# Window attention issued in the written order on four engines, as a pipeline of query steps

## Chip, cores and metric

The kernel runs on one core of one Trainium2 chip. The time is that of one execution on the device, in microseconds (us). The kernel before was run three times: 968.87, 969.32 and 969.57 us, median 969.32.

## What is computed

Causal attention over a window of 128 positions, with a linear bias per head, on 4 batches of 8 heads, 576 positions and head size 64. Then two feed-forward networks (FFNs) on the 2304 tokens, 512 to 2048 to 512, the first with a sigmoid gate and the second with a clipped square. The weights come as 64-bit floats.

```python
scores = q @ k.T / 8 - slope[h] * |i - j|      # only 0 <= i - j < 128, else -1e9
attn = exp(scores - max);  attn = attn / (sum(attn) + 1e-9)
x = (attn @ v) as (2304, 512)
h = x @ w1_in;  x = (h / (1 + exp(-1.702 h))) @ w1_out
h = x @ w2_in;  out = where(h >= 1, h, where(h <= -1, 0, (h + 1)**2 / 4)) @ w2_out
```

## The kernel before

Attention goes by **units**: one batch and two heads, 16 units. A unit has 9 groups of 64 queries, taken two at a time in five **steps** (m = 0 to 4; the last has one group), so there are 80 steps in all. A group's queries of both heads fill the 128 rows, and its keys are a strip of up to 192 columns (64 and 128 in a unit's first two groups).

Per unit, `trans_qk` (three chunks c) transposes q and k on TensorE and copies them out of PSUM: k on VectorE (DVE, line 206), q on ScalarE (ACT) or DVE (line 209). Per step, `scores` runs the score matmuls (line 220), then on DVE one operation that adds the bias, scales and takes the row's extreme (line 228), and on ACT the exp with its row sum (line 231). `norm` inverts the row sums on DVE (an add and a reciprocal, lines 238 and 239) and multiplies the probabilities on GpSimd (POOL, line 242). `trans_p` transposes the probabilities on TensorE and copies them out on ACT (lines 257 to 267). Per unit, `pv_unit` multiplies with v on TensorE (lines 281 to 287) and copies the result on ACT (line 288) and DVE (line 289) into `xt`, the activations that the FFN reads. The probabilities rotate through five buffers `pbuf`.

Beside attention, the first nine of 16 weight slices of the first FFN are loaded (`load_w1`, two halves each, 18 halves). A half is a DMA, five DVE operations that turn 64-bit floats into 32-bit ones (lines 65 to 73), a cast on ACT (line 75) and a subtraction on GpSimd (line 77) that leaves the rest, so that a value is kept as two parts.

The order of the work comes from keys. `at(key, fn, ...)` collects events, and they are traced in the order of their keys, counted in steps. What is traced is then put into each engine's queue by the planner of the language, which has a cost model and may put a later instruction that it holds ready ahead of an earlier one that waits. DMAs are issued by SyncE (SP), in a queue of their own. After the events, `split_block` cuts the first 462 tokens of `xt` into two parts for the FFN (ACT line 106, DVE line 107). In the FFN, every product of two such values is three matmuls (high by high, and twice high by low): `stage_h` (line 337) fills `ph`, ACT and DVE make `gs` (lines 343 to 351), and `stage_o` (lines 389 and 391) runs two stages behind. The other seven slices, and those of the second FFN, are loaded within the FFNs.

Of the kernel before, what the change touches and what calls it, by code (L numbers as in the profile page):

```python
# [25 lines left out]
def tile_window_attention_two_ffn(ctx: ExitStack, tc: tile.TileContext, q, k, v, w1_in, w1_out, w2_in, w2_out, out):  # L26
# [30 lines left out]
    def load_half(src, w, i, in_ffn=False):  # L57
        raw = stage.tile([P, 512, 2], I32, tag="raw", name="raw")
        if i == 0:
            nc.sync.dma_start(out=raw.rearrange("p (c f) t -> p c (f t)", c=KC), in_=src)  # L60
        else:
            nc.sync.dma_start(out=raw.rearrange("p f t -> p (f t)"), in_=src)
        lo, hi = raw[:, :, 0], raw[:, :, 1]
        x = stage.tile([P, 512], I32, tag="x", name="x", bufs=2)
        nc.vector.tensor_scalar(out=x, in0=hi, scalar1=0x7FFFFFFF, scalar2=None, op0=ALU.bitwise_and)
        nc.vector.tensor_scalar(
            out=f32(x), in0=f32(x), scalar1=HI_MIN, scalar2=HI_MAX, op0=ALU.max, op1=ALU.min)
        finish_late()
        nc.vector.tensor_scalar(
            out=x, in0=x, scalar1=3, scalar2=0x3FFFFFF8, op0=ALU.logical_shift_left, op1=ALU.bitwise_and)  # L70
        nc.vector.scalar_tensor_tensor(  # L71
            out=x, in0=lo, scalar=29, in1=x, op0=ALU.logical_shift_right, op1=ALU.bitwise_or)
        nc.vector.scalar_tensor_tensor(  # L73
            out=x, in0=hi, scalar=SIGN_TOP, in1=x, op0=ALU.bitwise_and, op1=ALU.bitwise_or)
        nc.scalar.copy(w[:, 0, i, :], f32(x))  # L75
# [18 lines left out]
    def load_w1(f, i):  # L94
        if i == 0:
            w1[f] = new_slice(w_a)
        load_weights(w1_in, w1_out, f, w1[f], (i,))
# [14 lines left out]
    with ExitStack() as actx:  # L112
# [80 lines left out]
        def trans_qk(u, c):  # L193
# [4 lines left out]
            ps = ps_a.tile([P, 2, 256], F32, tag="a", name="ps_qk")  # L198
            n = 256 if c < 2 else 64
            for i in range(2):  # L200
                for t in range(0, n, P):
# [3 lines left out]
                        ident[0:r, 0:r])  # L205
            nc.vector.tensor_copy(d["k"][:, 256 * c:256 * c + n], ps[:, 1, 0:n])
# [8 lines left out]
        def scores(u, m):  # L215
            b, hp = units[u]
            d = st[u]
            ps = ps_s.tile([P, 2, 256], F32, tag="s", name="ps_s")
            for e, i, lo in groups(m):
                nc.tensor.matmul(  # L220
                    ps[:, e, lo:192], d["q"][:, i, :], d["k"][:, 64 * i - 128 + lo:64 * i + 64], start=True, stop=True)
            n = NM * u + m
            assert n < len(pbuf) or n - len(pbuf) in done
            pt = d["p", m] = pbuf[n % len(pbuf)]
            sm = d["sm", m] = st_p.tile([P, 3, 2], F32, tag="sm", name="sm")
            for e, i, lo in groups(m):
# [3 lines left out]
                    scale=-0.125, scalar=3.0e38, accum_out=sm[:, 0, e:e + 1])  # L230
                nc.scalar.activation(  # L231
                    x, x, AF.Exp, bias=sm[:, 0, e:e + 1], scale=-1.0, accum_out=sm[:, 1, e:e + 1])

        def norm(u, m):
            d = st[u]
            sm, pt = d["sm", m], d["p", m]
            nn = len(groups(m))
            nc.vector.tensor_scalar_add(sm[:, 2, 0:nn], sm[:, 1, 0:nn], 1e-9)
            nc.vector.reciprocal(sm[:, 2, 0:nn], sm[:, 2, 0:nn])  # L239
            for e, i, lo in groups(m):  # L240
                x = pt[:, e, 64 * e + lo:64 * e + 192]
                nc.gpsimd.tensor_scalar(  # L242
                    out=x, in0=x, scalar1=sm[:, 2, e:e + 1], scalar2=1.0, op0=ALU.mult, op1=ALU.mult)

        def trans_p(u, m):
# [3 lines left out]
            if m == 0:  # L249
                d["pt"] = pt_p.tile([P, 4 * NM, P], F32, tag="pt", name="pt")  # L250
            pt = d["pt"]
            ps = ps_t.tile([P, 4, P], F32, tag="t", name="ps_t")
            n = 4 * m
            if m < NM - 1:
# [4 lines left out]
                if m > 0:  # L259
                    nc.scalar.copy(pt[:, n - 2:n + 2, :], ps)  # L260
                else:
                    nc.scalar.copy(pt[:, n:n + 2, :], ps[:, 2:4, :])  # L262
            else:
                nc.tensor.transpose(ps[:, 0, :], p[:, 0, 0:128], ident)  # L264
                nc.tensor.transpose(ps[0:64, 1, :], p[:, 0, 128:192], ident)
                nc.scalar.copy(pt[:, n - 2, :], ps[:, 0, :])
                nc.scalar.copy(pt[0:64, n - 1, :], ps[0:64, 1, :])

        def pv_unit(u):
            b, hp = units[u]  # L270
            d = st[u]
            pt, vr = d["pt"], d["v"]
            t0 = b * S
            heads = [slice(64 * j, 64 * j + 64) for j in range(2)]
            x = ps_x.tile([P, 512], F32, tag="x", name="ps_x")
            x1 = ps_a.tile([P, 2, 256], F32, tag="a", name="ps_x1")
# [11 lines left out]
            nc.scalar.copy(xt[hp][:, t0:t0 + 512], x)  # L288
            nc.vector.tensor_copy(xt[hp][:, t0 + 512:t0 + S], x1[:, 0, 0:64])
# [181 lines left out]
```

## Time and profile before

| | |
|---|---|
| median of 3 runs | 969.32 us |
| profiled execution | 969.63 us, span 967.8 us |
| busy: TensorE, weight loads | 954.2 us (99%), 841.2 us (87%) |
| busy: DVE, ACT, POOL | 564.9 us (58%), 383.5 us (40%), 99.2 us (10%) |
| first FFN matmul | 155.34 us from the span's start |

The profile is of one execution. Times in it count from the span's start. "Busy" is the time in which an engine had an instruction in work; instructions overlap at their ends, so the sum of durations is over the busy time, and a stretch that is shown as busy need not be dense. "Idle before" is the time in which the engine had nothing in work ahead of an instruction, with the releaser that ended it. PEld is TensorE's loading of weights (the stationary operand), PE its matmuls.

### The profile page before, as it was taken

To read this page: it belongs to the slowest core of one execution; us is meant where nothing else is said; L and a number is where in the kernel's file an instruction comes from. 1 tells how busy PE (TensorE), PEld (TensorE's weight loads), DVE (VectorE), ACT (ScalarE), POOL (GpSimd) and SP (SyncE) were. 2 spreads that over 40 slices of the span, in tenths; PEclk is the share of its full clock that TensorE was granted. 3 is DMA by queue.
4 is the path that set the end of the run, shared out by engine and by line. 5 is a ranking of instruction groups with operands and counts; after the bars stand their busy time and mean duration, and the time that the engine had idled before them with its cause. 6 is when DMAs were issued, how large, how long until landed. Compare 5 with 4: busy or idle time off the path is not lost.

```text
span 967.8 us, 13767 instructions
## 1 busy us (share of the span) xinstructions
PE 954.2 (99%) x5024; PEld 841.2 (87%) x5024; DVE 564.9 (58%) x1449; ACT 383.5 (40%) x928; POOL 99.2 (10%) x186
## 2 busy tenths in 40 slices
PE   7999999999999999999999999999999999999998
PEld 5878876888998989999888898899999999999997
DVE  5799999997323322422489999943443434444443
ACT  5999996333223222322333433332322422323322
POOL 4566664000000000000000000000000000000000
PEclk9999999999999999999999999999999999999999
DMA  5666644443000000000024333100000000000000
GB/s 135 156 156 163 154 124 121 131 131 109 1 1 1 1 1 1 1 0 1 1 80 133 118 105 113 63 33 1 17 16 1 33 1 1 33 1 1 33 1 33
DMA packets 81971, 53.32 MB, mean 55 GB/s; under 512 B 58992, under 2 KB 75632, under 8 KB 81904
## 3 DMA queue, kind: packets, MB, share of 16 engines
q1 hardware_dynamic: 81760, 52.31, 18.9%
q8 instruction: 40, 0.66, 0.3%
q14 instruction: 27, 0.22, 0.1%
q10 hardware_dynamic: 144, 0.13, 0.0%
HBM read 47.71 MB, written 4.72 MB: 54 GB/s over the span
## 4 chain that ended last, share of the span: by engine, by line
PE 93%; DVE 3%; SPq 1%; ACT 1%; DMA 1%; issue 0%; POOL 0%; POOLq 0%; ACTq 0%; DVEq 0%
PE ph L337 39%; PE o L389 21%; PE o L391 19%; PE ps_s L220 5%; PE ps_x L281 3%; PE ps_qk L203 2%; PE ps_t L257 1%; PE ps_t L258 1%; DVE x L73 1%; DVE x L71 1%; DMA raw<-in_moe_w_out_dram 0%; PE ps_x L287 0%; PE ps_t L264 0%; DVE w L79 0%; DVE ph L347 0%
## 5 line engine op out<-in xcount | busy, mean ns | idle before, releaser
L337 PE MATMUL ph<-xs,w 128*128 128x384 f32 (+2 forms) x2112 | 431.2, 353 | 0.0
L337 PEld LDWEIGHTS ph<-xs,w 128*128 128x128 f32 x2112 | 385.2, 188 | 28.7
L391 PE MATMUL o<-w,gs 128*128 128x512 f32 x864 | 216.5, 395 | 1.1 <-ACT gs L350 1.1
L389 PE MATMUL o<-gs,w 128*128 128x460 f32 (+1 forms) x960 | 213.8, 371 | 1.1 <-ACT gs L350 1.1
L389 PEld LDWEIGHTS o<-gs,w 128*128 128x128 f32 x960 | 180.5, 188 | 21.8 <-ACT gs L350 1.5
L391 PEld LDWEIGHTS o<-w,gs 128*128 128x128 f32 x864 | 161.0, 188 | 32.2 <-ACT gs L350 2.0
L350 ACT CAST gs<-ph 128x384 fp32r<-128x384 f32 (+2 forms) x176 | 89.7, 510 | 169.3 <-DVE ph L348 110.5
L351 DVE TENSOR_TENSOR gs<-ph,gs 128x384 fp32r<-128x384 f32 (+2 forms) x176 | 104.3, 593 | 73.4 <-ACT gs L350 73.1
L347 DVE TENSOR_TENSOR ph<-ph,ga 128x384 f32<-128x384 f32 x96 | 54.3, 565 | 143.4 <-ACT ga L346 143.4
L344 DVE TENSOR_TENSOR ph<-ph,ga 128x460 f32<-128x460 f32 (+1 forms) x80 | 51.4, 643 | 140.0 <-ACT ga L343 140.0
L346 ACT ACTIVATE ga<-ph,half 128x384 f32<-128x384 f32 x96 | 55.8, 582 | 155.2 <-PE ph L337 149.1
L343 ACT ACTIVATE ga<-ph 128x460 f32<-128x460 f32 (+1 forms) x80 | 44.4, 555 | 173.2 <-PE ph L337 173.1
L242 POOL TENSOR_SCALAR p<-p,sm 128x192 f32<-128x192 f32 (+1 forms) x144 | 70.0, 497 | 59.6 <-DVE sm L239 17.8
L231 ACT ACTIVATE p<-p,sm 128x192 f32<-128x192 f32 (+1 forms) x144 | 62.0, 433 | 8.9 <-DVE sm L228 8.5
L220 PE MATMUL ps_s<-kt,q 128*128 128x192 f32 (+2 forms) x288 | 60.4, 333 | 0.0
L75 ACT CAST w<-x 128x512 fp32r<-128x512 f32 x64 | 39.5, 620 | 44.8 <-DVE x L73 43.5
L348 DVE SCALAR_TENSOR_TENSOR ph<-ga,ph 128x384 f32<-128x384 f32 x96 | 53.8, 561 | 2.7
L228 DVE CUSTOM_DVE_ANT_0 p<-ps_s,bias 128x192 f32<-128x192 f32 (+1 forms) x144 | 44.9, 329 | 13.2 <-PE ps_s L220 8.9
L220 PEld LDWEIGHTS ps_s<-kt,q 128*128 128x128 f32 x288 | 45.3, 199 | 5.7 <-ACT pt L262 2.7
L71 DVE SCALAR_TENSOR_TENSOR x<-raw,x 128x512 int32<-128x512 int32 x64 | 45.1, 708 | 0.5
L73 DVE SCALAR_TENSOR_TENSOR x<-raw,x 128x512 int32<-128x512 int32 x64 | 44.7, 702 | 0.4
L281 PE MATMUL ps_x<-pt,vraw 128*64 128x256 f32 (+1 forms) x256 | 39.1, 366 | 0.3 <-ACT xt L288 0.3
(58 smaller groups left out, 589.0 us busy)
## 6 DMA issues: line engine op xcount, KB each, us to landing
raw<-in_moe_w_in_dram SPq DMA_DIRECT2D x32, 512.0 KB, 3.7
raw<-in_moe_w_out_dram SPq DMA_DIRECT2D x32, 512.0 KB, 3.5
out_dram<-ob SPq DMA_DIRECT2D x17, 256.0 KB, 2.0
vraw<-in_v_dram SPq DMA_DIRECT2D x32, 128.0 KB, 2.5
qkraw<-in_q_dram SPq DMA_DIRECT2D x30, 128.0 KB, 2.7
qkraw<-in_k_dram SPq DMA_DIRECT2D x30, 128.0 KB, 2.6
qkraw<-in_q_dram SPq DMA_DIRECT2D x16, 32.0 KB, 2.4
qkraw<-in_k_dram SPq DMA_DIRECT2D x16, 32.0 KB, 2.5
```

What stands on the lines that cost most here:

```text
L71: nc.vector.scalar_tensor_tensor(out=x, in0=lo, scalar=29, in1=x, op0=ALU.logical_shift_right, op1=ALU.bitwise_or)
L73: nc.vector.scalar_tensor_tensor(out=x, in0=hi, scalar=SIGN_TOP, in1=x, op0=ALU.bitwise_and, op1=ALU.bitwise_or)
L220: nc.tensor.matmul(ps[:, e, lo:192], d["q"][:, i, :], d["k"][:, 64 * i - 128 + lo:64 * i + 64], start=True, stop=True)
L231: nc.scalar.activation(x, x, AF.Exp, bias=sm[:, 0, e:e + 1], scale=-1.0, accum_out=sm[:, 1, e:e + 1])
L242: nc.gpsimd.tensor_scalar(out=x, in0=x, scalar1=sm[:, 2, e:e + 1], scalar2=1.0, op0=ALU.mult, op1=ALU.mult)
L281: nc.tensor.matmul(x[r, 128 * kb:128 * kb + 64 * n].rearrange("p (a b) -> p a b", b=64), vr[:, kb, r], pt[:, 4 * kb:4 * kb + n, r], start= ...
L337: nc.tensor.matmul(ph, w[f][:, a, 0, c * P:(c + 1) * P], xs[j][c][:, b, :], start=(c == 0 and i == 0), stop=(c == KC - 1 and i == 2))
L346: nc.scalar.activation(a, ph, AF.Relu, scale=0.5, bias=half)
L350: nc.scalar.copy(gs[:, 0, :], ph)
L351: act_last[0] = nc.vector.tensor_tensor(out=gs[:, 1, :], in0=ph, in1=f32(gs[:, 0, :]), op=ALU.subtract)
L389: nc.tensor.matmul(o[j][m][:, 0:n], w[f][:, a, 1, sl], gs[:, b, :], start=first, stop=last)
L391: nc.tensor.matmul(o[j][m], gs[:, b, sl], w[f][:, a, 1, :], start=first, stop=last)
```

## The change

Only the attention part is touched. All instructions of the events on TensorE, ACT, DVE and GpSimd are issued in the order in which they are traced, so the keys are now the order of these four queues. SyncE stays with the planner, and `setup` before the events and `split_block` behind them are outside.

The functions are cut so that each event has, by and large, the work of one engine at one point: `trans_qk` and `move_qk`, `scores` and `softmax`, `trans_p` and `move_p`, `pv_unit` and `move_x`. The keys move: scores one step ahead of their softmax, q/k transposes from 5u-1.58 to 5u-2.6, `trans_p` from s+3.5 to s+4.2, `pv_unit` from 5u+12.05 to 5u+13.2, loads of q/k from 5u-2.87 to 5u-4.6, loads of v from 5u-13.98 to 5u+3.5. The row sums of two steps share one small tile and are inverted together (`invert`), after which both steps are normalised; a unit's fifth step is inverted alone. A weight half becomes a generator in six pieces that are 0.55 step apart, and halves follow each other every 3.95 steps in place of 4.725.

```diff
-    def load_half(src, w, i, in_ffn=False):
+    def half_pieces(src, w, i, in_ffn=False):
...
         nc.vector.tensor_scalar(out=x, in0=hi, scalar1=0x7FFFFFFF, scalar2=None, op0=ALU.bitwise_and)
+        yield
...
+    def load_half(*args):
+        for _ in half_pieces(*args):
+            pass
...
+        def softmax(u, m):
...
+            if m % 2 == 0:
+                d["sm"] = st_p.tile([P, 3, 2, 2], F32, tag="sm", name="sm")
+            sm = d["sm", m] = d["sm"]
...
+        def invert(u, m):
+            d = st[u]
+            sm = d["sm", m].rearrange("p a b c -> p a (b c)")
+            nn = 4 if m < NM - 1 else 1
             nc.vector.tensor_scalar_add(sm[:, 2, 0:nn], sm[:, 1, 0:nn], 1e-9)
             nc.vector.reciprocal(sm[:, 2, 0:nn], sm[:, 2, 0:nn])
...
-                at(5 * u - 2.87, load_qk, u)
-                at(5 * u - 13.98, load_v, u)
+                at(5 * u - 4.6, load_qk, u)
+                at(5 * u + 3.5, load_v, u)
             for c in range(3):
-                at(5 * u - 1.58 + c * 1.49 if u > 0 else -99 + c, trans_qk, u, c)
+                key = 5 * u - 2.6 + c * 1.49 if u > 0 else -99 + c
+                at(key, trans_qk, u, c)
+                at(key + 0.45, move_qk, u, c)
             for m in range(NM):
                 s = 5 * u + m
-                at(s, scores, u, m)
-                at(s + 0.74, norm, u, m)
-                at(s + 3.5, trans_p, u, m)
-            at(5 * u + 4 + 8.05, pv_unit, u)
+                at(s - 1.0, scores, u, m)
+                at(s, softmax, u, m)
+                if m % 2 or m == NM - 1:
+                    at(s + 1.3, invert, u, m)
+                    at(s + 1.35, norm, u, m)
+                    if m % 2:
+                        at(s + 1.34, norm, u, m - 1)
+                at(s + 4.2, trans_p, u, m)
+                at(s + 4.7, move_p, u, m)
+            at(5 * u + 13.2, pv_unit, u)
+            at(5 * u + 14.1, move_x, u)
         for f in range(SPLIT):
             for i in range(2):
-                at(19.59 + 9.45 * (f + 0.5 * i), load_w1, f, i)
-        for key, _, fn, args in sorted(ev, key=lambda e: e[:2]):
-            fn(*args)
+                g = load_w1(f, i)
+                for n in range(6):
+                    at(19.59 + 3.95 * (2 * f + i) + 0.55 * n, next, g, None)
+        with tc.manual_schedule(engines={mybir.EngineType.PE, mybir.EngineType.Activation, mybir.EngineType.DVE,
+                                         mybir.EngineType.Pool}):
+            for key, _, fn, args in sorted(ev, key=lambda e: e[:2]):
+                fn(*args)
```

## Rows read from the trace of the kernel before

**Rows 1.** The page, busy time of each engine, its share, and instructions.

```profile
PE 954.2 (99%) x5024; PEld 841.2 (87%) x5024; DVE 564.9 (58%) x1449; ACT 383.5 (40%) x928; POOL 99.2 (10%) x186
```

**Rows 2.** Windows: stretch, length, busy PE, PEld, DVE, ACT, POOL (instructions), clock, DMA, GB/s.

```profile
18.70:26.60 7.90, 7.90 (x56) 6.03 (x55) 5.45 (x35) 7.76 (x29) 3.92 (x10) 1.00 0.73 158
43.60:132.50 88.90, 88.90 (x688) 70.75 (x687) 81.99 (x402) 83.37 (x293) 57.87 (x101) 1.00 0.63 157
...
200.00:240.00 40.00, 40.00 (x192) 35.89 (x191) 35.55 (x69) 15.10 (x27) 0.00 (x0) 1.00 0.38 120
240.00:968.00 728.00, 722.70 (x3542) 650.80 (x3540) 355.56 (x653) 216.98 (x404) 0.00 (x0) 1.00 0.08 27
```

**Rows 3.** Timeline at the FFN's start: start, duration, engine, line, count, idle before.

```profile
155.34 7.83 PE L337 MATMUL ph<-xs,w 128*128 128x462 f32 x36
...
164.28 2.80 PE L389 MATMUL o<-gs,w 128*128 128x462 f32 x12 [1.10 <-ACT gs L350]
```

**Rows 4.** Timeline of ACT within one unit, 90 to 98 us.

```profile
90.56 0.57 ACT L260 COPY pt<-ps_t 128x512 f32<-128x512 f32 x1
...
91.02 0.46 ACT L231 ACTIVATE p<-p,sm 128x192 f32<-128x192 f32 x1
...
91.47 0.45 ACT L231 ACTIVATE p<-p,sm 128x192 f32<-128x192 f32 x1
...
91.91 0.58 ACT L288 COPY xt<-ps_x 128x512 f32<-128x512 f32 x1
...
92.38 0.28 ACT L266 COPY pt<-ps_t 128x128 f32<-128x128 f32 x1
...
92.69 0.63 ACT L75 CAST w<-x 128x512 fp32r<-128x512 f32 x1
...
94.10 0.75 ACT L209 COPY q<-ps_qk 64x256 f32<-64x256 f32 x2
...
97.23 0.35 ACT L231 ACTIVATE p<-p,sm 128x64 f32<-128x64 f32 x1 [0.67 <-DVE sm L228]
```

**Rows 5.** Groups of DVE by line and shape, 43.6 to 132.5 us; last row 180 to 240.

```profile
L238 DVE TENSOR_SCALAR sm<-sm 128x2 f32<-128x2 f32 x40 | 7.7, 193 | 0.5 <-ACT p L231 0.5
L65 DVE TENSOR_SCALAR x<-raw 128x512 int32<-128x512 int32 x10 | 7.4, 743 | 0.0
L71 DVE SCALAR_TENSOR_TENSOR x<-raw,x 128x512 int32<-128x512 int32 x10 | 7.2, 722 | 0.0
L239 DVE RECIPROCAL sm<-sm 128x2 f32<-128x2 f32 x40 | 6.2, 155 | 0.1
L228 DVE CUSTOM_DVE_ANT_0 p<-ps_s,bias 128x64 f32<-128x64 f32 x11 | 2.4, 219 | 2.8 <-PE ps_s L220 1.7 <-POOL p L242 1.0
...
L65 DVE TENSOR_SCALAR x<-raw 128x512 int32<-128x512 int32 x13 | 5.5, 423 | 0.7 <-DMA raw<-in_moe_w_in_dram 0.6
```

**Rows 6.** The same view of ACT, 43.6 to 132.5 us: the exps.

```profile
L231 ACT ACTIVATE p<-p,sm 128x192 f32<-128x192 f32 x70 | 31.4, 452 | 1.3 <-DVE sm L228 1.3
...
L231 ACT ACTIVATE p<-p,sm 128x64 f32<-128x64 f32 x10 | 3.5, 348 | 2.1 <-DVE sm L228 2.0
```

**Rows 7.** Line 77 on GpSimd: ns min/median/max, first and last start in us.

```profile
L77 POOL TENSOR_TENSOR w<-x,w x18: 1262/1279/1716, 44.8 to 169.8; 128x512 fp32r<-128x512 f32 x18
```

**Rows 8.** Timeline of DVE at the start.

```profile
8.92 2.92 DVE L152 SCALAR_TENSOR_TENSOR bias<-rel,mask 64x192 bf16<-64x192 f32 x8
...
12.48 0.22 DVE L228 CUSTOM_DVE_ANT_0 p<-ps_s,bias 128x64 f32<-128x64 f32 x1
```

**Rows 9.** Timeline of DVE at the end of attention.

```profile
147.01 0.35 DVE L228 CUSTOM_DVE_ANT_0 p<-ps_s,bias 128x192 f32<-128x192 f32 x1
...
153.15 3.90 DVE L107 TENSOR_TENSOR xs<-xt,xs 128x462 fp32r<-128x462 f32 x3
```

**Rows 10.** Timeline of GpSimd and DVE at one weight half, 95 to 97 us.

```profile
95.05 1.72 POOL L77 TENSOR_TENSOR w<-x,w 128x512 fp32r<-128x512 f32 x1
...
95.67 1.38 DVE L69 TENSOR_SCALAR x<-x 128x512 int32<-128x512 int32 x1
```

More of the change, by code (lines that the diff above doesn't have):

```diff
@@ L96, in load_w1 @@
             w1[f] = new_slice(w_a)
-        load_weights(w1_in, w1_out, f, w1[f], (i,))
+        src = w1_out[f * P:(f + 1) * P, :]
+        if i == 0:
+            src = w1_in.rearrange("(c p) f -> p c f", p=P)[:, :, 2 * f * P:2 * (f + 1) * P]
+        yield from half_pieces(src, w1[f], i)
     NX = max(B1 + B2)
@@ L205, in trans_qk, with move_qk @@
                         ident[0:r, 0:r])
+        def move_qk(u, c):
+            d = st[u]
+            ps, n = d["ps", c], 256 if c < 2 else 64
             nc.vector.tensor_copy(d["k"][:, 256 * c:256 * c + n], ps[:, 1, 0:n])
@@ L215, in scores @@
         def scores(u, m):
-            b, hp = units[u]
             d = st[u]
-            ps = ps_s.tile([P, 2, 256], F32, tag="s", name="ps_s")
+            ps = d["s", m] = ps_s.tile([P, 2, 256], F32, tag="s", name="ps_s")
             for e, i, lo in groups(m):
@@ L221, in scores @@
                     ps[:, e, lo:192], d["q"][:, i, :], d["k"][:, 64 * i - 128 + lo:64 * i + 64], start=True, stop=True)
+        def softmax(u, m):
+            b, hp = units[u]
+            d = st[u]
+            ps = d["s", m]
             n = NM * u + m
@@ L229, in scores @@
                     out=x, in0=ps[:, e, lo:192], in1=bias[:, hp, lo:192], op0=ALU.add, op1=ALU.min,
-                    scale=-0.125, scalar=3.0e38, accum_out=sm[:, 0, e:e + 1])
+                    scale=-0.125, scalar=3.0e38, accum_out=sm[:, 0, m % 2, e:e + 1])
                 nc.scalar.activation(
-                    x, x, AF.Exp, bias=sm[:, 0, e:e + 1], scale=-1.0, accum_out=sm[:, 1, e:e + 1])
+                    x, x, AF.Exp, bias=sm[:, 0, m % 2, e:e + 1], scale=-1.0, accum_out=sm[:, 1, m % 2, e:e + 1])
+        def invert(u, m):
+            d = st[u]
+            sm = d["sm", m].rearrange("p a b c -> p a (b c)")
+            nn = 4 if m < NM - 1 else 1
+            nc.vector.tensor_scalar_add(sm[:, 2, 0:nn], sm[:, 1, 0:nn], 1e-9)
+            nc.vector.reciprocal(sm[:, 2, 0:nn], sm[:, 2, 0:nn])
         def norm(u, m):
@@ L258, in trans_p @@
                     nc.tensor.transpose(ps[:, 2 + e, :], p[:, e, 128:256], ident)
[L259 to L262, printed above, removed]
             else:
@@ L265, in trans_p, with move_p @@
                 nc.tensor.transpose(ps[0:64, 1, :], p[:, 0, 128:192], ident)
+        def move_p(u, m):
+            d = st[u]
+            if m == 0:
+                d["pt"] = pt_p.tile([P, 4 * NM, P], F32, tag="pt", name="pt")
+            pt, ps, n = d["pt"], d["t", m], 4 * m
+            if m == 0:
+                nc.scalar.copy(pt[:, n:n + 2, :], ps[:, 2:4, :])
+            elif m < NM - 1:
+                nc.scalar.copy(pt[:, n - 2:n + 2, :], ps)
+            else:
                 nc.scalar.copy(pt[:, n - 2, :], ps[:, 0, :])
@@ L269, in pv_unit @@
         def pv_unit(u):
-            b, hp = units[u]
             d = st[u]
             pt, vr = d["pt"], d["v"]
-            t0 = b * S
             heads = [slice(64 * j, 64 * j + 64) for j in range(2)]
-            x = ps_x.tile([P, 512], F32, tag="x", name="ps_x")
-            x1 = ps_a.tile([P, 2, 256], F32, tag="a", name="ps_x1")
+            x = d["x"] = ps_x.tile([P, 512], F32, tag="x", name="ps_x")
+            x1 = d["x1"] = ps_a.tile([P, 2, 256], F32, tag="a", name="ps_x1")
             last = NM - 1
@@ L287, in pv_unit, with move_x @@
                 nc.tensor.matmul(x1[r, 0, 0:64], vr[0:64, last, r], pt[0:64, 4 * last - 1, r], start=False, stop=True)
-            nc.scalar.copy(xt[hp][:, t0:t0 + 512], x)
-            nc.vector.tensor_copy(xt[hp][:, t0 + 512:t0 + S], x1[:, 0, 0:64])
+        def move_x(u):
+            b, hp = units[u]
+            d = st[u]
+            t0 = b * S
+            nc.scalar.copy(xt[hp][:, t0:t0 + 512], d["x"])
+            nc.vector.tensor_copy(xt[hp][:, t0 + 512:t0 + S], d["x1"][:, 0, 0:64])
         ev = []
```

18 lines of the change are left out of this document (7 added, 11 removed).

## Prediction

> **What bounds the kernel now.** I read the page first: TensorE shows 99% of the span busy [rows 1], which alone says nothing, since it is drawn busy in attention and in the FFNs alike. So I read the windows next [rows 2]. In the FFN stretches weight loads (PEld) fill 35.89 of 40 us and the matmul count is steady (192 in 40 us; 3542 in 728 us, 4.87 per us). That is TensorE at its own pace, nothing in the diff touches it, and it begins at 155.34 us [rows 3]. In the ten attention units from 43.60 to 132.50 the same column is only 70.75 of 88.90, while ACT is busy 83.37 and DVE 81.99 [rows 2]. So the span is 155.3 us of attention in front of an 812 us FFN stretch, and only the first part, with its seam to the second, can move.
>
> A rule of the Trainium skill bears on that column. It (Perfetto Trace Analysis, section "Identifying the Most-Contended Engine") says that matmul busy share is a bad measure of how near TensorE is to its limit, and that busy weight loads tell more. The two rows above agree, 80% against 90%. By the matmul column alone nothing could be gained in attention, which is rival 1.
>
> Next I read the timeline of ACT in one unit, to get what an instruction costs there from its start to the start of the next [rows 4]. A 192-wide exp with its sum read takes 0.45 us (91.02 to 91.47), a 512-wide copy 0.46 (90.56 to 91.02), the output copy 0.47 (91.91 to 92.38), the two last small copies 0.31 together (92.38 to 92.69), two q copies 0.75. One unit is 7 wide exps 3.15, the 64-wide 0.35, the 128-wide about 0.40, three wide copies 1.38, the 256-wide copy about 0.27 (between the small and the wide ones), the two small 0.31, three q copies 1.12, the output copy 0.47: together 7.45 us. A weight half adds one cast, 0.63 less the 0.10 by which such copies overlap the next, 0.52. The stretch ran one half per unit (10 in 88.9 us [rows 5]), so ACT needed 7.97 of the 8.89 us that a unit took. **ACT is the nearest bound, and 0.92 us per unit are lost to waits.** Of these the profile shows 3.4 us in ten units as idle time before exps, nearly all for DVE, and 2.1 of it in front of the first, 64-wide exp of a unit [rows 6]. DVE itself sat idle 2.8 us before that same first step, 1.7 of it for the score matmuls [rows 5]: a unit's first scores come just in time, after transposes and copies of q and k.
>
> **The change, part by part.**
>
> *Lead.* Scores are issued one step before their softmax, q/k transposes about one step earlier (key 5u-2.6 for 5u-1.58), and their copies become events of their own. This takes away the wait at a unit's start. In the other places DVE still feeds ACT, but the order now lets DVE be about a step ahead. I take the 0.34 us of shown waits as gone, and 0.1 of the hidden rest: 0.92 becomes about 0.47. Bounds: 0.1 (all hidden) and over 0.92 (rival 2). What then is late next is DVE itself.
>
> *Row sums for two steps.* Per unit five adds and five reciprocals become three of each. They last 0.193 and 0.155 us [rows 5], so four fewer save DVE at most 0.70 us of busy time; much of such a duration overlaps the next, so I take 0.4, lower end 0.28. The inversion now stands behind both exps of the pair, so the even step is normalised about 1.6 steps later (key 2.34 for 0.74). GpSimd waits, the transposes of that step behind it are moved from 3.5 to 4.2, and after the later normalisation 1.9 steps (3 us) remain for some 1.7 us of GpSimd work. I cost that wait at nothing; if its cover goes, TensorE's transposes, the copies and the probability buffer five steps on stall by the excess, up to one weight subtraction (1.28 us at the median [rows 7]).
>
> *Weights.* Halves come every 3.95 steps instead of 4.725, cut into six pieces. From step 20 to 80 that is 15.2 halves in 12 units, 1.27 a unit instead of 1. ACT: +0.27 x 0.52 = 0.14. GpSimd: +0.27 x 1.28 = 0.35, against 57.87 busy of 88.90. DVE: a half is three single-input operations and two two-input ones; undisturbed, as later in the FFN, the first kind takes 0.42 and the second about 0.7, 2.7 us in all, and here up to 0.74 and 0.72, 3.7 us [rows 5]. I take 3.2, so +0.86 us per unit (0.7 to 1.0). DVE goes from 8.20 busy to 8.20 - 0.4 + 0.86 = 8.66, though that column counts stalls and overlaps. The five DVE pieces are spread 0.55 step apart, so a step waits behind one or two pieces, not five. What is gained is at the far end: in before the subtractions of these halves run until 169.8 us [rows 7], far into the FFN.
>
> *Unit time.* ACT 7.45 + 1.27 x 0.52 = 8.11, plus waits 0.47, is 8.58; I take **8.6 us**, which also sits at the DVE figure. Units 0 to 3 carry no weights: ACT 7.45, and the window of unit 1, also without, took 7.90 [rows 2]. I take 7.75 (7.6 to 7.9) for each of units 1 to 3.
>
> *Start.* The first step's DVE operation is at 12.48, behind 2.92 us of bias set-up that began at 8.92 [rows 8]. Whether the set-up now precedes the first copies, the trace can't tell; 10.5 to 12.5, I take 11.8. The first unit has no copies of probabilities to do: 5.8 us (it took 6.2).
>
> *Loads.* SyncE is not in the list of ordered engines, so its queue stays with the planner. Loads of q and k keep three buffers, and those of v still wait for the product two units back, which is 1.15 steps later in the order now (13.2 for 12.05) with its own use later by as much; in the first units q and k go ahead of v, which favours the start. I cost it at nothing; if v were late TensorE would wait at the product, and everything behind it with it.
>
> *Tail.* In before the last step's DVE operation starts at 147.01 and the first FFN matmul at 155.34, 8.3 us later. Now behind the last step stand five copies, the output of unit 14 and the product of unit 15, about 7.2 us through ACT and the single output bank; and on DVE 13 weight pieces, about 8 us, with the split of the first token block last in the written order. In before the planner drew its DVE part forward, three subtractions of 1.3 us each from 153.15 [rows 9]; if it may not do so past the ordered region, the FFN is held up to 10 us after the last step. I take 8.4.
>
> *FFN seam.* TensorE waited 1.10 us for gs at 164.28 [rows 3], while weight halves left from attention occupied DVE. These are gone: -1.1, and -0.4 for a slightly slower pace until 240 us (192 in 40 us against 4.87 per us is under 3 matmuls). Together 1.5 us.
>
> **Sum.** 11.8 + 5.8 + 3 x 7.75 + 11.8 units x 8.6 (steps 20 to 79) = 142.3 us for the last step; + 8.4 = 150.7 for the FFN, against 155.3: 4.6 us. With the seam 6.1 us. The profiled run took 969.63 with a span of 967.8, and the median of the three runs is 969.32; 969.4 - 6.1 = **963.3 us**.
>
> **Rivals.**
>
> 1. *TensorE, or ACT and DVE together, already bound a unit at 8.9 to 9.1 us.* For: the full matmul column, and ACT and DVE both over 92% busy [rows 2]. Against: the PEld share. With 9.0 a unit the last step is 4.7 us later: 968.0, no difference.
>
> 2. *Strict order on DVE makes it the bound (slower).* In before a blocked weight operation is followed by whatever is ready. Now a softmax step queued behind a piece waits for it, and behind a pair's inversion DVE waits for ACT's second exp. A 512-wide DVE operation took 1.38 us instead of 0.42 while GpSimd ran its 1.72 us subtraction [rows 10], and the first exp of a unit, next in line behind it, found ACT idle for 0.67 us [rows 4]. With 1.27 such blocks of 0.95 us per unit unhidden, over the 8.3 to 8.4 us of the rest, a unit takes about 9.6 us: 963.3 + 11.8 x 1.0 = 975.1. It is slower than before from a unit of 9.1 us on, and measurably from 9.3. The Trainium skill (SBUF — State Buffer, section "Who interferes with whom") has the rule for it: the port pair that VectorE and GpSimd share is an exclusive lock, and the loser blocks for the whole instruction. The 1.38 us row agrees with it. Against the rival: six short pieces instead of a run of five, and a step of lead.
>
> 3. *The pipeline runs at ACT's pace.* 8.2 a unit, start at 10.5, first unit 5.5, then 7.6 each, tail 7.2: 135.6 + 7.2 = 142.8, 12.5 us earlier, with the seam 14: 955.4.
>
> **How the numbers follow.** Forecast (959 to 967) 0.55; rival 3 0.12; rival 1 0.15; rival 2 0.18. Under 0.2%, 1.9 us, a measurement of this kernel can't be told from no change: faster 0.67, same 0.15, slower 0.18. The range reaches from most of the way to rival 3 up to the mild half of rival 2: 957 to 972, which leaves about 0.07 below and 0.13 above.
>
> **What would show it.** Right: the first FFN matmul near 151 us; units from the fourth on spaced 8.6 us; idle time before the 64-wide exp near zero; no weight subtraction on GpSimd after the FFN's first microseconds; no wait for gs near the FFN's start. Wrong: units over 9 us with exps waiting for DVE behind weight pieces (rival 2); GpSimd's normalisation as what transposes wait for (pair inversion); a gap between the last product and the first FFN matmul (tail); or a first FFN matmul that moves while the end doesn't.

## Result and profile after

The changed kernel is slower: 979.08 us at the median of three runs (978.85, 979.08, 981.16), against 969.32 us; the ratio is 1.0108 [1.0085, 1.0131]. The profiled run took 978.85 us with a span of 977.1. The forecast was 963.3 us, so it missed by 15.8 us and on the other side of no change; its range ended at 972.

The page of the kernel after, the line that answers to [rows 1]:

```profile
PE 948.7 (97%) x5024; PEld 839.4 (86%) x5024; DVE 561.6 (57%) x1385; ACT 384.3 (39%) x928; POOL 103.7 (11%) x186
```

64 DVE instructions are gone with the inversions, and every other count is the same. As before, this line can't say where the time went. The time stamps of a unit's first step and of the FFN's first matmul can. The table lays both profiles side by side (us from the span's start):

| | before | after | after less before |
|---|---|---|---|
| first step of unit 4 | 43.6 | 42.2 | -1.4 |
| first step of unit 15 (11 units later) | 141.5 | 147.3 | +5.8 |
| last step | 147.01 | 153.16 | +6.15 |
| first FFN matmul | 155.34 | 166.04 | +10.70 |
| end of the span | 967.8 | 977.1 | +9.3 |

So units 0 to 3 gained 1.4 us, the 11 units with weights lost 7.2 (9.55 us each for 8.90), the last unit 0.3, the **tail** (last step to FFN) 4.6 (12.9 for 8.3), and the FFN gained 1.4 (811.1 for 812.5). The windows show the two parts that lost, with the columns of [rows 2]. First the kernel before, over the same 11 units and the tail:

```profile
43.60:141.50 97.90, 97.90 (x756) 77.74 (x755) 89.61 (x442) 91.62 (x322) 64.28 (x112) 1.00 0.62 156
147.00:155.30 8.30, 7.34 (x62) 4.15 (x60) 8.16 (x23) 6.60 (x19) 6.35 (x7) 1.00 0.42 113
```

Then the kernel after: the 11 units, the longest of them, and the tail:

```profile
42.20:147.30 105.10, 94.96 (x752) 77.02 (x750) 95.97 (x416) 94.49 (x326) 72.58 (x113) 0.98 0.59 149
70.20:83.00 12.80, 11.03 (x75) 9.07 (x74) 9.60 (x40) 10.02 (x33) 8.33 (x14) 0.87 0.59 157
153.20:166.00 12.80, 8.82 (x64) 5.28 (x64) 8.82 (x20) 6.13 (x19) 7.85 (x10) 0.87 0.39 110
```

Per unit, DVE is busy 95.97 / 11 = 8.72 us and ACT 94.49 / 11 = 8.59, in a unit of 9.55. On average both have over 0.8 us of idle time in a unit, and neither is more than 92% busy. The loss is uneven. Unit 7, the window from 70.2 us, took 12.7 us for 8.7 before, so that 4.0 of the 7.2 us lie in it; the other ten units took 9.23 us in the mean, for 8.91, and in these DVE is idle for 0.59 us and ACT for 0.78. What sets unit 7 apart stands in the last section. What each waited for stands in the groups (line, operation, shape, count, busy us, mean ns, idle before and what ended it). DVE and ACT of the kernel after, 42.2 to 147.3 us, to set beside [rows 5] and [rows 6]:

```profile
L250 DVE CUSTOM_DVE_ANT_0 p<-ps_s,bias 128x192 f32<-128x192 f32 x77 | 24.5, 351 | 3.7 <-PE ps_t L283 2.5 <-POOL p L268 0.4 <-PE ps_t L280 0.3
L74 DVE SCALAR_TENSOR_TENSOR x<-raw,x 128x512 int32<-128x512 int32 x14 | 10.0, 717 | 0.2
L65 DVE TENSOR_SCALAR x<-raw 128x512 int32<-128x512 int32 x15 | 9.7, 645 | 0.0
L260 DVE TENSOR_SCALAR sm<-sm 128x4 f32<-128x4 f32 x22 | 5.6, 252 | 2.8 <-ACT p L253 2.8
...
L253 ACT ACTIVATE p<-p,sm 128x192 f32<-128x192 f32 x77 | 34.5, 450 | 5.7 <-DVE sm L250 5.3
L225 ACT COPY q<-ps_qk 64x256 f32<-64x256 f32 x34 | 12.5, 367 | 3.0 <-DVE q L225 1.1 <-DVE kt L222 1.0 <-PE ps_qk L215 0.5
L253 ACT ACTIVATE p<-p,sm 128x64 f32<-128x64 f32 x11 | 3.8, 350 | 0.6 <-DVE sm L250 0.6
```

The wait that the change was to remove, before a unit's 64-wide exp, is gone (0.6 us, where [rows 6] have 2.1). It came back in front of the wide exps (5.7 for 1.3), and DVE now waits for ACT at the inversion of a pair (2.8). The two engines wait for each other in turn. One such turn, in unit 8, timeline of DVE in the kernel after:

```profile
83.32 0.14 DVE L260 TENSOR_SCALAR sm<-sm 128x1 f32<-128x1 f32 x1
83.49 0.16 DVE L261 RECIPROCAL sm<-sm 128x1 f32<-128x1 f32 x1
83.57 0.44 DVE L71 TENSOR_SCALAR x<-x 128x512 int32<-128x512 int32 x1
83.93 0.20 DVE L222 COPY kt<-ps_qk 128x64 f32<-128x64 f32 x1
84.06 0.45 DVE L225 COPY q<-ps_qk 64x64 f32<-64x64 f32 x2
84.54 0.69 DVE L74 SCALAR_TENSOR_TENSOR x<-raw,x 128x512 int32<-128x512 int32 x1
85.26 0.36 DVE L250 CUSTOM_DVE_ANT_0 p<-ps_s,bias 128x192 f32<-128x192 f32 x1
...
90.69 0.17 DVE L260 TENSOR_SCALAR sm<-sm 128x4 f32<-128x4 f32 x1 [1.07 <-ACT p L253]
```

and of TensorE and ACT in the same stretch:

```profile
80.66 0.82 PE L235 MATMUL ps_s<-kt,q 128*128 128x192 f32 x4
...
85.66 0.46 ACT L253 ACTIVATE p<-p,sm 128x192 f32<-128x192 f32 x1 [1.15 <-DVE sm L250]
...
87.91 0.60 ACT L80 CAST w<-x 128x512 fp32r<-128x512 f32 x1
88.42 0.58 ACT L293 COPY pt<-ps_t 128x512 f32<-128x512 f32 x1
88.90 0.74 ACT L225 COPY q<-ps_qk 64x256 f32<-64x256 f32 x2
89.67 0.46 ACT L253 ACTIVATE p<-p,sm 128x192 f32<-128x192 f32 x1
```

The scores of the step at 85.26 were done at 81.5. From 83.32 on DVE does, in the written order, an inversion, a weight piece, copies of k and q and another weight piece, 1.94 us in which ACT runs dry for 1.15 us. Five microseconds later it is DVE that stands at the pair's inversion for 1.07 us, since ACT still had a cast and copies to do ahead of the exp at 89.67. The pieces that could have filled this wait are queued behind it.

### The profile page after: what moved, and what is told of

Its sections match the earlier page's. It is cut to its first block, busy times and chain, and to the rows that moved or that the text cites. A ratio compares the mean times of both kernels' runs of the same rounds, so it can differ in the third digit from the quotient of the medians.

```text
span 977.1 us, 13644 instructions
## 1 busy us (share of the span) xinstructions
PE 948.7 (97%) x5024; PEld 839.4 (86%) x5024; DVE 561.6 (57%) x1385; ACT 384.3 (39%) x928; POOL 103.7 (11%) x186
## 4 chain that ended last, share of the span: by engine, by line
PE 79%; DVE 10%; ACT 6%; DMA 2%; issue 2%; SPq 0%; POOL 0%; DVEq 0%; POOLq 0%; ACTq 0%
PE ph L382 37%; PE o L436 20%; PE o L434 17%; ACT p L253 3%; DMA raw<-in_moe_w_in_dram 2%; DVE x L74 1%; PE ps_x L308 1%; PE ps_s L235 1%; DVE x L77 1%; DVE p L250 1%; ACT q L225 1%; ACT pt L293 1%; DVE x L65 1%; DVE w L84 1%; DVE x L71 1%
## 5 line engine op out<-in xcount | busy, mean ns | idle before, releaser
L392 DVE TENSOR_TENSOR ph<-ph,ga 128x384 f32<-128x384 f32 x96 | 54.2, 565 | 142.9 <-ACT ga L391 142.9
L268 POOL TENSOR_SCALAR p<-p,sm 128x192 f32<-128x192 f32 (+1 forms) x144 | 74.5, 534 | 39.7 <-ACT p L253 12.9
L253 ACT ACTIVATE p<-p,sm 128x192 f32<-128x192 f32 (+1 forms) x144 | 61.9, 432 | 10.4 <-DVE sm L250 9.9
L250 DVE CUSTOM_DVE_ANT_0 p<-ps_s,bias 128x192 f32<-128x192 f32 (+1 forms) x144 | 42.1, 327 | 7.9 <-PE ps_t L283 6.2
L215 PE MATMUL ps_qk<-ident,qkraw 128*128 128x128 f32 (+1 forms) x160 | 27.1, 283 | 9.3 <-DMA qkraw<-in_q_dram 4.1
```

The costliest lines, as they stand in the source:

```text
L253: nc.scalar.activation(x, x, AF.Exp, bias=sm[:, 0, m % 2, e:e + 1], scale=-1.0, accum_out=sm[:, 1, m % 2, e:e + 1])
L268: nc.gpsimd.tensor_scalar(out=x, in0=x, scalar1=sm[:, 2, m % 2, e:e + 1], scalar2=1.0, op0=ALU.mult, op1=ALU.mult)
L392: nc.vector.tensor_tensor(out=ph, in0=ph, in1=a, op=ALU.max)
```

## Experiments

All medians stand beside runs of the kernel before on the same chip (968.7 to 969.9 us); ratios are to these. "u4 to u15" is the mean unit over the 11 units from the first step of unit 4 to that of unit 15, "tail" the time from the last step to the first FFN matmul.

| kernel | us | ratio [95%] | u4 to u15 | last step | tail |
|---|---|---|---|---|---|
| before | 969.3 | 1 | 8.90 | 147.0 | 8.3 |
| after | 979.08 | 1.0108 [1.0085, 1.0131] | 9.55 | 153.2 | 12.9 |
| planner_order | 972.46 | 1.0033 [1.0022, 1.0043] | 8.86 | 146.4 | 10.6 |
| dve_free | 970.69 | 1.0021 [1.0011, 1.0030] | 8.72 | 143.6 | 13.2 |
| light_halves | 965.14 | 0.9960 [0.9945, 0.9975] | 8.57 | 142.3 | 8.8 |
| light_planner | 964.74 | 0.9958 [0.9943, 0.9973] | 8.63 | 143.8 | 8.6 |
| slow_weights | 979.65 | 1.0112 [1.0096, 1.0127] | 9.03 | 149.6 | 14.0 |
| three_qk_banks | 987.08 | 1.0189 [1.0168, 1.0211] | 9.88 | 160.9 | 11.8 |
| six_buffers | 978.80 | 1.0088 [1.0072, 1.0105] | 9.45 | 151.4 | 13.8 |
| product_behind | 978.56 | 1.0092 [1.0077, 1.0108] | 9.57 | 153.1 | 12.8 |
| single_inversion | 978.19 | 1.0086 [1.0071, 1.0102] | 9.56 | 153.6 | 10.6 |
| before_pairs | 976.26 | 1.0079 [1.0064, 1.0094] | 9.40 | 153.3 | 8.4 |
| order_on_before | 1023.75 | 1.0552 [1.0536, 1.0567] | 12.63 | 200.7 | 7.9 |
| tail_free | 976.31 | 1.0076 [1.0059, 1.0093] | 9.44 | 152.0 | 12.1 |
| planner_single | 969.42 | 1.0001 [0.9992, 1.0010] | 9.13 | 148.0 | 8.2 |
| dve_tail_free | 967.66 | 0.9985 [0.9975, 0.9994] | 8.71 | 142.9 | 11.7 |
| dve_tail_single | 965.69 | 0.9963 [0.9948, 0.9977] | 8.74 | 143.5 | 9.3 |

### Is it the order? planner_order, dve_free

planner_order is the changed kernel without the ordered region; dve_free keeps it on three engines.

```diff
-        with tc.manual_schedule(engines={mybir.EngineType.PE, mybir.EngineType.Activation, mybir.EngineType.DVE,
-                                         mybir.EngineType.Pool}):
+        with tc.manual_schedule(engines={mybir.EngineType.PE, mybir.EngineType.Activation, mybir.EngineType.Pool}):
```

> The changed kernel without the strict order on the four engines: the planner may reorder again; keys, cut-up functions, pair inversion and the weights' pace stay. If strict order is what costs (theory A), units fall from 9.55 to 8.9 us or less, the first FFN matmul comes at 150 to 156 us and the time is 964 to 970 us. If the denser weight halves on DVE are what costs (theory B), units stay over 9.3 us and the time is 975 to 980 us.

> The changed kernel with DVE taken out of the strict order (TensorE, ACT and GpSimd keep it). Theory F (DVE is the engine that sets a unit's time, busy 91% of it in every run so far, and fixed places for its weight pieces are what costs): units at 9.0 us or less, 970 to 975 us. Theory G (the coupling of TensorE, ACT and GpSimd to each other costs, whatever DVE does): units stay over 9.3, 977 to 981 us.

The written order costs 979.1 - 972.5 = 6.6 us, and the order **on DVE** 979.1 - 970.7 = 8.4 us; on the other three alone it costs nothing that the time shows (970.25 to 972.13 us, and 970.42 to 973.42 without it). planner_order's units fell as theory A said, but its time came 2.5 us above that theory's range, since its tail is still 10.6 us. Window of dve_free's 11 units, and its group of wide exps there:

```profile
41.20:137.10 95.90, 91.16 (x752) 75.74 (x751) 90.46 (x408) 92.80 (x324) 70.21 (x113) 1.00 0.65 164
```

```profile
L253 ACT ACTIVATE p<-p,sm 128x192 f32<-128x192 f32 x77 | 34.7, 454 | 0.7 <-DVE sm L250 0.3
```

ACT is 97% busy, for 90% in the kernel after, and its wide exps wait 0.7 us in all where they waited 5.7. DVE's idle time falls from 0.83 to 0.49 us per unit. Its work falls as well, from 8.72 to 8.22, since the planner lets weight pieces slip behind attention's operations: 12 or 13 of each kind in these 11 units, for 14 or 15 in the kernel after. The rest is done in the tail, which is 13.2 us long.

### Is it DVE's load? light_halves, light_planner, slow_weights

light_halves leaves four of the five DVE operations of each weight half in attention out (the slices then do not hold the weights); light_planner does that without the ordered region. slow_weights spaces the halves as before.

```diff
-                    at(19.59 + 3.95 * (2 * f + i) + 0.55 * n, next, g, None)
+                    at(19.59 + 4.725 * (2 * f + i) + 0.55 * n, next, g, None)
```

> The changed kernel with four of the five DVE operations of each weight half left out in attention (the first FFN's first nine slices are then not the weights); the DMA, the first operation, the cast and the subtraction stay. Theory B: DVE loses about 2.2 us per half, 2.8 a unit, ACT becomes the bound at 8.1 to 8.4 us a unit, first FFN matmul at 146 to 152 us, 959 to 966 us. Theory C (TensorE waits for ACT's q copies, because transposes and products share two PSUM buffers, and DVE's load is not the point): units stay at 9.0 us or more, 973 us or more.

> The kernel with light weight halves (four of the five DVE operations of a half left out in attention, so that the first FFN's first nine slices are not the weights) without the strict order. Strict, it took 965.1 us with units of 8.6 us and ACT busy 98% of them. Theory F: with DVE's load gone, strict order is no dearer than the planner's: 963 to 968 us. Theory G: strict order costs here too, and without it the time is 955 to 961 us.

> The changed kernel with weight halves every 4.725 steps, as before the change, in place of 3.95; all else stays. Theory B (DVE full of weight pieces): 0.27 halves a unit less, each 2.7 to 3.3 us on DVE, so 0.7 to 0.9 us a unit less and 969 to 972 us. Theory A (strict order couples the engines whatever the load): at most 0.3 us a unit, 975 to 979 us, since the halves left over then run at the start of the FFN.

Without the weights' DVE work the written order costs nothing that shows (965.14 against 964.74 us), with it 6.6 to 8.4: it is the two together. (The operations left out are also ones that can run beside a GpSimd subtraction and be held up by it; these two runs don't separate such blocks from DVE's load as such.) Window of light_halves:

```profile
42.40:136.70 94.30, 90.87 (x752) 75.63 (x750) 66.97 (x359) 92.18 (x325) 57.55 (x113) 1.00 0.68 171
```

DVE is busy for 71%, and ACT for 92.18 / 94.30 = 98%, which is how full ACT gets once DVE always has the next step ready; a unit still takes 8.57 us. slow_weights gained 0.5 us per unit, over half of it in unit 7 (9.4 us for 12.7), and lost it again, so that its time is in neither theory's range: the last step came 3.5 us earlier, but halves that were put off filled the tail (14.0 us) and the FFN's first stretch (814.5 us to the end, for 811.1). Moving this work within attention is no gain by itself.

### Is it a buffer or a bank? three_qk_banks, six_buffers, product_behind

TensorE waited 4.1 us for ACT's copies of q to free a bank, DVE 2.5 for a probability buffer, and the transposes of a unit's fifth step, which free such a buffer, stood in TensorE's queue behind the product of the unit before. The edits: `ps_a` 3 and `ps_s` 2 banks in place of 2 and 3; six `pbuf` for five; `pv_unit` at 5u+13.3 for 13.2.

> The changed kernel with three PSUM buffers for q/k transposes and the products' last columns in place of two, and two for scores in place of three. Theory C: TensorE's waits for q copies ahead of q/k transposes (4.1 us shown in ten units, and what follows from them) go, units fall by 0.4 us or more, 972 to 976 us. Theories A and B: no change within 1.5 us of 979, or slower, since scores have one buffer less of lead.

> The changed kernel with six probability buffers in place of five; orders are the same. Theory D: softmax no longer waits for the transposes behind the product, units as in the run with the product behind, tail unchanged: 973 to 977 us. Theory B: 978 to 981 us.

> The changed kernel with one key moved, pv_unit from 5u+13.2 to 5u+13.3, so that on TensorE the transposes of a unit's fifth step go ahead of the 2 us product block of the unit before, not behind it. Theory D (the product block holds up the transposes that free a probability buffer, so the fourth or fifth softmax step waits): DVE's waits for these transposes (6.2 us in four visible ones, up to 1.9 each) go, units fall by 0.3 us or more, and the tail, where the product of unit 14 stood ahead of the last transposes, by 1 to 3 us: 970 to 976 us. Theory B (DVE's own load under strict order): no change in units, 977 to 980 us.

None of them is the cause. The third q/k bank, paid for with one of the scores, made it 8 us slower: TensorE waited 9.5 us before score matmuls for DVE to free a bank, where the kernel after has 0.2. The scores' lead of a step needs the third bank. With six buffers unit 7 took 11.7 us in place of 12.7, but in tail_free, which has the order and the five buffers of the kernel after up to the last step, it took 11.5, so this isn't shown to come from the buffer; the time fell by nothing that shows. product_behind left units and tail as they were.

### The inversion for two steps: single_inversion, before_pairs, planner_single

single_inversion and planner_single (without the ordered region) invert every step's row sums by themselves again; before_pairs is the kernel before with only the inversion for two steps.

```diff
-                if m % 2 or m == NM - 1:
-                    at(s + 1.3, invert, u, m)
-                    at(s + 1.35, norm, u, m)
-                    if m % 2:
-                        at(s + 1.34, norm, u, m - 1)
+                at(s + 1.3, invert, u, m)
+                at(s + 1.35, norm, u, m)
```

> The changed kernel with the row sums inverted step by step again (five adds and five reciprocals a unit), each 1.3 steps behind its softmax; strict order and all else stay. Theory E (the pair inversion sends GpSimd four normalisations at once and makes them and the transposes late): GpSimd's and TensorE's waits behind the inversion shrink, the tail falls by 1 us or more, 974 to 977 us. Theory B (DVE's load counts): 0.3 to 0.7 us a unit more, 982 to 988 us.

> The kernel before with one part of the change alone: row sums inverted for two steps at once, the even step normalised with the odd one. Planner's order, keys and weights' pace as before. Theory F (DVE sets the unit's time at about 91% busy): 0.4 us of DVE work less a unit, units fall by 0.3 to 0.4 us, 963 to 967 us. Rival: the even step's probabilities come a step later and TensorE's transposes wait for them, 969 to 973 us.

> The changed kernel with all engines left to the planner (as planner_order, 972.5 us), and every step's row sums inverted by themselves. Theory P1: the inversion for two steps, which cost 7.6 us in the kernel before (before_pairs), is also what makes planner_order 3.2 us slower than the kernel before; without it 965 to 969 us. Theory P2: with the changed keys the normalisation has time, and the 3.2 us come from the denser weights and the tail; 972 us or more.

In the kernel before, the inversion for two steps alone costs 976.26 - 968.66 = 7.6 us, which neither expectation had. Window of before_pairs, and then the first three of its waits in it (engine, line, waited for, us in total, times, longest):

```profile
44.50:147.90 103.40, 101.48 (x754) 78.10 (x755) 84.40 (x401) 92.51 (x321) 59.52 (x113) 1.00 0.59 148
```

```profile
POOL p L248 <- DVE sm L241: 16.4, 11, 2.2
DVE p L230 <- PE ps_s L220: 8.7, 18, 0.9
ACT p L233 <- DVE sm L230: 6.2, 10, 1.0
```

DVE does less (84.40 of 103.40 us) and everything takes longer: GpSimd stands 16.4 us for the inverted sums, and the keys around it are those for a normalisation one step earlier. In the changed kernel, whose keys give more room, it costs 972.46 - 969.42 = 3.0 us under the planner and 0.9 us under the written order (977.76 to 978.30 us, for 978.85 to 981.16). In both pairs of profiles the tail is what gets shorter without it, 10.6 to 8.2 and 12.9 to 10.6 us, while the last step comes later, by 1.6 and 0.5 us. Under the written order the pairs buy nothing within the units either: DVE is busy for 101.07 / 11 = 9.19 us of a unit in single_inversion and 8.72 in the kernel after, yet a unit takes 9.56 and 9.55 us, so what is saved comes back as idle time (0.37 and 0.83). single_inversion's tail fell as theory E said, but its time is in neither range. How much of planner_single's 3.0 us lies in the tail its profile can't settle: the two profiled spans differ by 0.6 us only. The new keys with the cut functions and the denser weights, without pairs and without order, are worth what the kernel before is: planner_single's ratio is 1.0001. Without pairs the written order costs 978.19 - 969.42 = 8.8 us, so the pairs are not what makes it dear.

### The order alone: order_on_before

The kernel before, with its events inside the ordered region and nothing else changed.

> The kernel before, with nothing changed but that the four engines issue in the written order. Theory A (strict order costs by itself, unless the functions are cut up for it): here the copies stand directly behind their transposes and softmax directly behind its scores, so every step waits for TensorE: units over 10 us, 990 us or more. If strict order costs little by itself and the new keys do the harm: 969 to 975 us.

With the functions and keys of before the order costs 54 us. From 40 to 180 us its longest waits on DVE are 27.2 us at the sums for ACT's exp, and GpSimd waits 36.1 us for ACT's casts. The cut into pieces and the new keys thus take back most of what the order costs, and not all.

### The tail: tail_free, dve_tail_free, dve_tail_single

tail_free ends the ordered region at key 79.5, dve_tail_free does so on top of dve_free, and dve_tail_single also inverts every step by itself.

```diff
+                if key < 79.5:
+                    fn(*args)
+        for key, _, fn, args in order:
+            if key >= 79.5:
                 fn(*args)
```

> The changed kernel with the strict order ending behind the last softmax step (key 79.5); what comes later is the planner's. The tail, from the last step's DVE operation to the first FFN matmul, was 12.9 us under strict order, 10.6 with the planner throughout and 8.3 in the kernel before. If strict order makes the tail long: 9 to 10.5 us, first FFN matmul at 162 to 164, 974 to 977 us. If the weight halves left at that point do, whoever orders them: 12 us or more, 978 to 980 us.

> The changed kernel with the written order kept on TensorE, ACT and GpSimd alone (DVE left to the planner, as in dve_free), and on those three only for keys below 79.5, that is up to the last step; everything with a later key is left to the planner. Theory T1 (the long stretch between the last step and the first FFN matmul, 13.2 us in dve_free, comes from the strict order of what stands there): it falls to 10.6 us, as in planner_order, the last step stays at about 143.6 us, so about 968.0 us. Theory T2 (it comes from the weight work that is left over and from TensorE's clock at its half level there, whatever the order): 12 us or more, 969.5 to 971 us.

> As dve_tail_free, with the row sums of every step inverted by themselves (an add and a reciprocal each, five per unit, and normalisation right behind them). Theory P1 (the inversion for two steps delays the normalisation, and with DVE's order free that is what a unit waits for): units of 8.5 us or less in place of 8.72 and a tail that is 1 to 2 us shorter, 963 to 966 us. Theory P2 (four short DVE instructions more per unit, 0.4 us by the forecast's estimate, fill an engine that is already busy for 0.95 of the stretch): units of 8.9 us or more, 970 us or more.

Timeline of the end of attention in the kernel after, rows of GpSimd, DVE and TensorE:

```profile
153.87 1.26 POOL L82 TENSOR_TENSOR w<-x,w 128x512 fp32r<-128x512 f32 x1
153.96 1.20 DVE L260 TENSOR_SCALAR sm<-sm 128x4 f32<-128x4 f32 x1 [0.30 <-ACT p L253]
...
155.54 3.49 POOL L268 TENSOR_SCALAR p<-p,sm 128x192 f32<-128x192 f32 x5 [0.41 <-DVE sm L261]
...
159.06 3.20 PE L308 MATMUL ps_x<-pt,vraw 128*64 128x256 f32 x16
...
164.00 1.74 PE L308 MATMUL ps_x<-pt,vraw 128*64 128x256 f32 x16 [0.99 <-ACT xt L320]
```

Four things lie in a row. The last pair's inversion runs into GpSimd's weight subtraction and takes 1.20 us, where this add had 0.25 in the mean; five normalisations behind it end at 159.03; the product of unit 14 runs at TensorE's lower clock, 3.20 us for a block that takes 1.74 at full clock; and the last product waits 0.99 us for the one output bank. (The Trainium skill, SBUF — State Buffer, section "Who interferes with whom", says that where a VectorE instruction uses the port pair that it shares with GpSimd, whoever of the two issues first gets the pair for the whole instruction, and the other fully blocks. The rows agree: the add ends 0.03 us after the subtraction.)

Four kernels with the same keys set the tail out by two of its causes. Without order and pairs it is 8.2 us (planner_single), as in the kernel before; with pairs alone 10.6 (planner_order), with the order alone 10.6 (single_inversion), with both 12.9. So each adds 2.3 to 2.5 us, the order's part with the clock in it: the granted clock of the tail is 1.00 in the first two and 0.84 and 0.87 in the ordered ones. Each of these is one profile.

Letting the tail out of the order gained 2.8 us (tail_free) and 3.0 (dve_tail_free), yet the tail shrank only by 0.8 and 1.5 us; the rest came ahead of it, in dve_tail_free 0.7 us by the last step. Its 11.7 us lie between what the two theories said, though its time is that of the first (968.0). With single inversion the tail is 9.3 us and the clock there 1.00. Window of dve_tail_free's tail:

```profile
142.90:154.60 11.70, 9.27 (x64) 5.25 (x63) 8.45 (x19) 5.82 (x17) 8.05 (x10) 0.85 0.47 147
```

and the units and the tail of dve_tail_single:

```profile
41.10:137.20 96.10, 91.61 (x754) 75.83 (x753) 93.82 (x454) 92.98 (x326) 70.23 (x112) 1.00 0.67 165
143.50:152.80 9.30, 7.54 (x64) 4.56 (x63) 9.09 (x20) 5.98 (x19) 7.29 (x9) 1.00 0.53 151
```

**dve_tail_single, 965.69 us, beats both kernels**: 0.4% under before, 1.4% under after. Its units, 8.74 us, are neither the 8.5 nor the 8.9 that the two theories gave: the earlier normalisation gains nothing that shows there, and the four short DVE instructions more per unit cost next to nothing (the last step is 0.6 us later). DVE is busy for 93.82 / 96.10 = 98% of them, so a DVE that may take what is ready can be filled.

## Why the prediction was wrong, point by point

The miss of 15.8 us is, by the profile: start and first units 1.35 (unit 4 was to begin at 40.85 us and began at 42.2), units 9.5 (101.5 forecast from there to the last step, 110.96 measured), tail 4.5, seam 0.1, and 0.4 in the baseline and the median.

- **Unit time, the step that failed.** "ACT 7.45 + 1.27 x 0.52 = 8.11, plus waits 0.47, is 8.58; I take 8.6 us, which also sits at the DVE figure." The two sums were near right: DVE was to be busy 8.66 us and was 8.72, and ACT's busy column rose by 0.26 us (8.33 to 8.59) for 0.14. (Each has the split of the first token block in it, which ran within these units: three operations, 1.9 us in all on DVE and 1.7 on ACT.) The use of them was wrong. A unit of 8.6 us asks DVE to be busy for all of it, when before it was idle (97.90 - 89.61) / 11 = 0.75 us per unit, and gives it an order in which it can't step past a wait. Two engines that feed each other, each busy for 92 to 94% [rows 2], didn't overlap to 100%: measured 0.83 idle on DVE, 0.96 on ACT, 9.55 in all. The idle time of DVE was put at nothing, without a row. It is 0.59 us in the ten units beside unit 7, which take 9.23; unit 7 alone, with 3.2 us, brings the mean up to 9.55; of the 4.0 us that it lost, 1.25 are the clock (last section). dve_free (8.72) and light_halves (8.57) show that the order and DVE's load, together, are the cause of most of it.
- **Lead.** "In the other places DVE still feeds ACT, but the order now lets DVE be about a step ahead." The wait at a unit's start went as forecast; the total before the exps rose, from 3.4 us in ten units [rows 6] to 6.3 in eleven.
- **Row sums for two steps.** The saving was right, 0.51 us per unit (18.4 to 12.8 us over 11 units) for 0.4. "I cost that wait at nothing" was wrong. Within the units it ate the saving (single_inversion), and it shows most in the tail, which is 2.3 to 2.4 us shorter without it in three pairs of kernels (after and single_inversion, planner_order and planner_single, dve_tail_free and dve_tail_single).
- **Weights.** 1.29 halves per unit and 3.14 us of DVE for each (9.7 + 8.9 + 6.4 + 10.0 + 9.6 over 14.2), for 1.27 and 3.2: right. That "a step waits behind one or two pieces, not five" is what the timeline shows at 83.57 and 84.54, but I gave it no price.
- **Start.** 12.58 us for 11.8: the bias set-up of 2.93 us at 9.02 still stands ahead of the first step, as before [rows 8]. Units 1 to 3 took 8.0 us in the mean, for 7.75.
- **Tail.** The thing I feared, the split held back, didn't happen: its subtractions on DVE ran between 34.2 and 61.9 us, where before they stood at 153.15 [rows 9]. 8.4 became 12.9 by the inversion for two steps and the written order, in about equal parts, with the clock's fall in the second; the denser weights alone left it at 8.2 (planner_single). The wait for the one output bank was named, and is 0.99 us.
- **FFN seam.** -1.5 forecast, -1.4 measured; the 1.10 us wait of [rows 3] is gone.
- **Rivals.** Rival 2 has the right sign and place, with 9.6 us a unit for 9.55 and 975.1 us for 979.1. That its number fits is in part luck. Its price was taken from blocks by GpSimd, which got no longer: a half took 3.14 us on DVE, and 3.31 in the kernel before (the means of its five operations, over the 11 units); and the ten units beside unit 7 took 9.23. What the timelines show is the other half of it, steps queued behind pieces and behind the pair's inversion. I gave it 0.18 and held "six short pieces" and "a step of lead" against it, and took neither from a row. Rival 1 falls with dve_free and light_halves, whose units take under 8.9 us with the same matmuls; the 8.2 us of rival 3 no kernel reached.

**What stays open.** What the order adds to the tail is not split between the weight pieces, the queues and the clock, since each moves the others. Nor was it tried to keep attention's DVE operations in the written order while only the weight pieces stay free.

## What to carry to other kernels

Where two engines feed each other and both are busy for over 90% of a stage, add the idle time that each has now to its busy time, and ask what would remove it; a sum of busy time is a floor, not a forecast. Fixing the order of an engine takes away its filling of waits, and here that cost most on the engine that carries both the critical steps and background work: fix the order on its neighbours, and leave that one free (dve_free, dve_tail_single). Batching a small operation to save its fixed cost also delays everyone who waits for the first of the batch, so look at the consumer, and at the end of the stage, before counting the saving.

## What the runs showed of the hardware

TensorE's clock fell to its lower level (1.2 of 2.4 GHz) in a stage that the page shows as nearly always busy. In the kernel after this was in unit 7 and in the tail, with granted clocks of 0.87 over 12.8 us each, and of 0.50 from 74 to 75 us. Timeline of TensorE around the first of them:

```profile
71.28 0.92 PE L235 MATMUL ps_s<-kt,q 128*128 128x192 f32 x4 [0.62 <-ACT q L225]
73.02 0.33 PE L279 MATMUL ps_t<-ident,p 128*128 128x128 f32 x1 [0.82 <-POOL p L268]
...
73.90 1.49 PE L235 MATMUL ps_s<-kt,q 128*128 128x192 f32 x4
```

Two waits of under a microsecond each stand ahead of it, and then four score matmuls take 1.49 us for 0.92. It is tempting to call the waits the reason. tail_free speaks against it: up to its last step it has the same order as the kernel after, and its other units take the same time to within 0.02 us. It has the same two waits, and its clock stayed at full:

```profile
71.31 0.92 PE L235 MATMUL ps_s<-kt,q 128*128 128x192 f32 x4 [0.63 <-ACT q L225]
73.05 0.33 PE L279 MATMUL ps_t<-ident,p 128*128 128x128 f32 x1 [0.82 <-POOL p L268]
...
73.72 0.82 PE L235 MATMUL ps_s<-kt,q 128*128 128x192 f32 x4
```

So these waits don't suffice, and what brings the clock down stays open. The pair of profiles gives the price: unit 7 took 12.72 us with the fall and 11.47 without it, 1.25 us. In the tail the product's block took 3.20 us for 1.74. The kernel before shows no fall in its profile; order_on_before has a mean granted clock of 0.977 over its whole span.

The rest of unit 7 is a wait of another kind. Timeline of GpSimd in the kernel after:

```profile
70.92 1.47 POOL L82 TENSOR_TENSOR w<-x,w 128x512 fp32r<-128x512 f32 x1 [2.47 <-ACT w L80]
72.37 2.41 POOL L268 TENSOR_SCALAR p<-p,sm 128x192 f32<-128x192 f32 x5
```

The sums of the pair were inverted by 69.69 us, but in the written order their normalisation stands behind a weight subtraction that waits for ACT's cast, and TensorE's transposes then wait for it (0.82 us). dve_free and light_halves, which keep this order on GpSimd, have their longest unit here too (10.1 and 10.4 us), and planner_order and light_planner, which don't, take 8.5 and 8.6. So the order on the other three engines may not be free in every unit, though the time as a whole shows no cost of it. This is read from timelines and not tested by a run of its own; dve_tail_single, which keeps that order and inverts every step by itself, took 8.4 us there.
